# Two fp32 load pairs split into partition halves over two DMA queues, and four more output stores cut in two, in a fused channel-attention and MLP kernel

## The chip, the cores and the metric

The kernel runs on one core of a Trainium2 chip. The metric is device time in microseconds (us) of that core, as the median of several executions. The kernel before takes 713.97 us (three executions, 713.9 to 714.35); the profiled execution has a span of 712.6 us.

## What is computed

Channel attention (XCiT style) over four batches of 6080 tokens and 256 channels, and then a two-layer MLP with a squared-ReLU activation over all 24,320 tokens.

```python
qn = q / (norm(q, axis=1) + 1e-6);  kn = k / (norm(k, axis=1) + 1e-6)   # norms over the 6080 tokens
s  = kn.T @ qn / tau                       # 256 x 256 for each batch
a  = softmax-like exp(s - max) / sum       # per row
x  = v @ a                                 # (24320, 256)
h  = x @ w_in                              # 256 -> 2048
out = (s * relu(h)**2 + b) @ w_out         # 2048 -> 256, fp32
```

Inputs and outputs are fp32. The products on the chip are done in fp16 with fp32 accumulation.

## The kernel before, in words

**Two phases.** The attention matrix of a batch is folded into the first MLP weight (`wa = a @ w_in`, one 256 x 2048 matrix for each batch), so that the tokens pass through two matrix products only. A batch's matrix needs all its tokens of q and k. For batch 0 nothing can hide that: q and k are loaded, their Gram matrix and norms are summed, the softmax and the fold are done, and only then does the token loop start. I call this stretch the head. The token loop goes over `NG` = 48 groups of 512 tokens (the last has 256); the Gram matrices of batches 1 to 3 are computed inside it.

**The head.** Batch 0 is cut into 13 chunks: eleven of 128 partitions x 4 rows, one of 128 x 2 and one of 96 x 2. A chunk has a k and a q part, each 512 KB of fp32 in memory for a full chunk. `Gram.load` (L119) issues them. For the first `NDIRECT` = 2 chunks the parts go uncast into the fp32 tile `raw32` (L131): k on SyncE's queue, q on ScalarE's queue. `Gram.cast` (L136) then converts them to fp16 into the chunk's `qk` tile: k on VectorE (L139), q on ScalarE (L140). All other chunks are issued on GpSimd's queue (L133), where the transfer itself casts to fp16. `qk_pool` has eight buffers. Behind the loads of batch 0 GpSimd's queue has the first group of v (L453), the pieces of w_in (L512), and then w_out and more of v.

For each chunk TensorE does eight matmuls into `s_ps` (L149), which need both parts of the chunk. Squares of k and q are taken on ScalarE (L180) and VectorE (L177), folded on VectorE (L194) and summed into one row block (L208). The last three chunks (`NLATE` = 3) are handled apart: k's squares first, then the norms by ones-matmuls (L247, L251), the inverse norms on ScalarE (L272), the scaling of `s_ps` (L297), the exponentials (L303), the fold of the first weight columns (L347, L324, L326). The first matmul of the token loop is `h_ps` (L751). `keep_busy` (L544) adds a few idle matmuls late in the head.

**The token loop.** A group has 16 steps. Each step does two matmuls of the first product (L751); its result is taken out by ScalarE as ReLU (L761) and squared on VectorE or ScalarE (L774, L772). The second product of a group runs one group later: seven products of half size in place of eight (`seven_items`, L922), with sums of blocks on VectorE (L849 to L855). VectorE scales and adds the result into `o_sb` (L779), and `store` (L786) sends it to memory on SyncE's queue. v is loaded by GpSimd (L453) and transposed by DMA on SyncE's queue (L475), some 26 steps before its use.

**Order.** Every compute instruction and most transfers are kept in program order on their engine. The two direct loads (L131) are not, but nothing waits ahead of them: each stands at the start of its queue. A `store` waits on SyncE's queue until VectorE has written its part of `o_sb`, and the transposes of a later group of v stand behind it.

**Stores.** In `p3` and `p4` of `seven_items`, a group in `HALVES` (L838) is stored in two parts: columns of rows 0 and 1 of each partition after the sixth product, rows 2 and 3 after the seventh. Any other group is stored in one transfer after the seventh. Both kinds cover all 128 partitions.

Of the kernel before, what the change touches and what calls it, by code (L numbers as in the profile page):

```python
# [17 lines left out]
def kernel(  # L18
# [12 lines left out]
    nc = tc.nc  # L31
    P = 128
# [16 lines left out]
    NG = (NT + TG - 1) // TG  # L49
# [6 lines left out]
    def po(ins):  # L56

        tc.keep_in_program_order(ins)
        return ins
# [52 lines left out]
    class Gram:  # L112
# [7 lines left out]
        def load(self, c, parts=(0, 1)):  # L120

            at, np_, jc = self.chunks[c]
            if 0 in parts:
                self.raw[c] = qk_pool.tile([P, 2, JC, C], FP16, tag="qk", name="qk")
            t = self.raw[c]
            direct = self.b == 0 and c < NDIRECT
            for i in parts:
                src = (k, q)[i]
                rows = src[self.b, at : at + np_ * jc, :].rearrange("(p j) c -> p j c", j=jc)
                if direct:  # L130
                    (nc.sync, nc.scalar)[i].dma_start(out=raw32[:, c, i], in_=rows)  # L131
                else:
                    po(nc.gpsimd.dma_start(out=t[:np_, i, :jc, :], in_=rows))  # L133
            self.tiles[c] = t[:, 1], t[:, 0]
# [356 lines left out]
    raw32 = gpool.tile([P, NDIRECT, 2, JC, C], FP32, tag="g16", name="raw32")  # L491
# [166 lines left out]
    for i, f in enumerate(folds):  # L658
        early.setdefault(FOLDS[i], []).append(f)
    at_step(14, lambda: po(nc.vector.tensor_scalar_mul(  # L660
        out=s_out, in0=s_bc, scalar1=1.0 / (LAM * LAM))))
# [114 lines left out]
    def evacuate(dst, src, add, n):  # L776
        if n == 1:
            add = add[:, None, :].broadcast_to((P, 2, add.shape[-1]))
        po(nc.vector.scalar_tensor_tensor(out=dst, in0=src, scalar=s_out, op0=ALU.mult,  # L779
                                          in1=add, op1=ALU.add))  # L780

    def store(g, j0=0, j1=None, cols=slice(0, C), queue=nc.sync):
        t0, nj = group(g)
        o_sb = o_sbs.pop(g) if j1 is None else o_sbs[g]
        j1 = nj if j1 is None else j1
        po(queue.dma_start(  # L786
            out=out[t0 : t0 + nj * P, :].rearrange("(p j) d -> p j d", j=nj)[:, j0:j1, cols],
            in_=o_sb[:, j0:j1, cols]))
# [46 lines left out]
                    store(g)  # L835


    HALVES = (1, 2, 3, NG - 2)  # L838
    S = {}

    def sums_of(g, n, i0=0, i1=NP):
# [15 lines left out]
    def seven_items(g):  # L857
# [6 lines left out]
        def out_sb(t, half):  # L864
            if g not in o_sbs:
                o_sbs[g] = opool.tile([P, TG // P, C], FP32, tag="o_sb", name="o_sb")
            return o_sbs[g][:, ts(t, 2), half]
# [19 lines left out]
        def p3():  # L887
            evacuate(out_sb(0, hi), st["Z"], st["u2"], 2)
            if g in HALVES:
                store(g, 0, 2)  # L890

        def p4():
            evacuate(out_sb(1, lo), st["X"], rowconst[:, lo], 1)
            store(g, 2 if g in HALVES else 0)

# [123 lines left out]
```

## Time and profile before

| | value |
|---|---|
| time, median of 3 | 713.97 us |
| span of the profiled execution | 712.6 us |
| busy TensorE, VectorE, ScalarE, GpSimd | 97%, 89%, 77%, 16% |
| first matmul of the head | 7.56 us |
| first matmul of the token loop | 37.59 us |
| DMA busy share, 0 to 60 us | 0.9 or more from 2 us on |
| moved by DMA in the whole span | 83.81 MB |
| store, 512 KB, SyncE's queue: issue to landing | 3.0 us (43 of them) |
| store, 256 KB, SyncE's queue: issue to landing | 5.9 us (8 of them) |

The busy shares are means over the whole span. The head and the token loop have different limits, so the views are read for each of them apart. In the view of the chain that ended last, each line is a start, a duration and what filled it; in the view of waits, each line is who waited, for whom, the sum in us, the number of waits and the longest.

### The profile page before, as it was taken

The numbers are of one execution on the slowest core, as the hardware profiler recorded it, in microseconds if no ns is written. First come the engines' busy times: TensorE is split into PE (matmuls) and PEld (weight loads), VectorE is DVE, ScalarE is ACT, GpSimd is POOL, SyncE is SP. The second block draws the span as 40 slices with busy tenths as digits, with TensorE's granted clock in tenths as the row PEclk, the third lists the DMA queues.
The fourth block names the chain that finished last, engine by engine and source line by source line (L and its number), as shares of the span: only waits on it lengthen the run. The fifth ranks groups of instructions, "written<-read, shape, count | busy, mean of one in ns | idle before, by whom it ended". The sixth has DMA issues, their size and how long they took to land.

```text
span 712.6 us, 17529 instructions
## 1 busy us (share of the span) xinstructions
PE 693.7 (97%) x7422; PEld 502.7 (71%) x7422; DVE 635.1 (89%) x905; ACT 548.8 (77%) x599; POOL 113.7 (16%) x192
## 2 busy tenths in 40 slices
PE   3799999999999999999999999999999999999998
PEld 2556777776777777777677777777768777777777
DVE  4889999999988989998999899998998888888886
ACT  5789877787777777778877777777876777777875
POOL 4533042202101222111010222111000000000000
PEclk9899999999999999999999999999999999999999
DMA  9999998557655977465761889737323333321202
GB/s 234 207 258 174 166 176 140 111 105 122 128 113 105 138 139 147 106 96 101 153 130 50 149 136 148 128 76 99 99 64 75 95 71 75 97 61 46 83 31 75
DMA packets 87838, 83.81 MB, mean 118 GB/s; under 512 B 56352, under 2 KB 62768, under 8 KB 87760
## 3 DMA queue, kind: packets, MB, share of 16 engines
q0 software_dynamic: 26992, 43.74, 38.2%
q1 hardware_dynamic: 60192, 37.71, 22.1%
q8 instruction: 58, 0.95, 0.5%
q10 hardware_dynamic: 576, 1.25, 0.5%
q14 instruction: 20, 0.16, 0.1%
HBM read 78.91 MB, written 24.90 MB: 146 GB/s over the span
## 4 chain that ended last, share of the span: by engine, by line
PE 95%; DMA 3%; ACT 1%; DVE 1%; issue 0%; DVEq 0%; ACTq 0%
PE h_ps L751 46%; PE o_ps L922 40%; PE s_ps L149 4%; DMA qk<-in_k_dram 1%; PE wa_ps L389 1%; DMA raw<-in_q_dram 1%; PE o_ps L826 1%; ACT sq L180 1%; PE o_ps L798 0%; PE wa_ps L331 0%; DVE f L194 0%; ACT r L272 0%; PE n_ps L247 0%; ACT qk L140 0%; DVE f L208 0%
## 5 line engine op out<-in xcount | busy, mean ns | idle before, releaser
L761 ACT ACTIVATE r<-h_ps 128x1024 f16<-128x1024 f32 (+1 forms) x384 | 388.8, 1014 | 143.8 <-PE h_ps L751 140.3
L751 PE MATMUL h_ps<-vT,wa 128*128 128x512 f16 (+7 forms) x1632 | 452.0, 364 | 0.5 <-ACT wa L324 0.5
L922 PEld LDWEIGHTS <-S 128*128 128x128 f16 x2944 | 198.1, 98 | 84.3
L922 PEld LDWEIGHTS <-g 128*128 128x128 f16 x2208 | 155.0, 98 | 74.0
L774 DVE TENSOR_TENSOR g<-r 128x2048 f16<-128x2048 f16 (+2 forms) x150 | 174.4, 1163 | 10.2 <-ACT r L761 9.7
L922 PE MATMUL o_ps<-T,S 128*128 128x128 f16 x2208 | 183.1, 219 | 0.0
L751 PEld LDWEIGHTS <-wa 128*128 128x128 f16 x1632 | 136.6, 98 | 19.0 <-ACT wa L324 1.0
L922 PE MATMUL o_ps<-w_out,g 128*128 128x128 f16 x1472 | 134.2, 219 | 0.0
L772 ACT ACTIVATE g<-r 128x1024 f16<-128x1024 f16 (+1 forms) x97 | 100.3, 1034 | 0.2
L779 DVE SCALAR_TENSOR_TENSOR o_sb<-o_ps,s_out,u 128x256 f32<-128x256 f32 x138 | 66.2, 480 | 36.1 <-PE o_ps L922 34.3
L149 PE MATMUL s_ps<-qk 128*128 128x256 f16 (+1 forms) x384 | 71.8, 289 | 13.9 <-ACT qk L140 9.4
L453 POOL DMA_DIRECT2D v<-in_v_dram x48 | 31.4, 663 | 238.7 <-DMA vT<-v 173.8
L210 POOL DMA_DIRECT2D f<-f x33 | 28.9, 875 | 248.4 <-DVE f L194 201.5
L779 DVE SCALAR_TENSOR_TENSOR u<-o_ps,s_out,rowconst 128x256 f32<-128x256 f32 x138 | 65.7, 476 | 0.0
L922 PE MATMUL o_ps<-w_out,S 128*128 128x128 f16 x736 | 63.5, 219 | 0.0
L922 PE MATMUL o_ps<-N,g 128*128 128x128 f16 x736 | 63.4, 219 | 0.0
L180 ACT ACTIVATE sq<-qk 128x1024 f16<-128x1024 f16 (+2 forms) x53 | 54.5, 1041 | 3.9 <-DMA qk<-in_k_dram 2.4
L851 DVE TENSOR_TENSOR S<-S,g 128x2048 f16<-128x2048 f16 (+1 forms) x47 | 56.4, 1200 | 1.2
L849 DVE TENSOR_TENSOR S<-g 128x2048 f16<-128x2048 f16 (+1 forms) x47 | 56.0, 1192 | 0.0
L855 DVE TENSOR_TENSOR S<-g,S 128x2048 f16<-128x2048 f16 x46 | 55.9, 1214 | 0.0
L853 DVE TENSOR_TENSOR S<-g 128x2048 f16<-128x2048 f16 x46 | 55.8, 1214 | 0.0
L149 PEld LDWEIGHTS <-qk 128*128 128x128 f16 (+1 forms) x384 | 32.9, 103 | 20.4 <-ACT qk L140 9.9
(103 smaller groups left out, 335.1 us busy)
## 6 DMA issues: line engine op xcount, KB each, us to landing
out_dram<-o_sb SPq DMA_DIRECT2D x43, 512.0 KB, 3.0
v<-in_v_dram POOLq DMA_DIRECT2D x47, 256.0 KB, 4.6
qk<-in_k_dram POOLq DMA_DIRECT2D x42, 256.0 KB, 6.4
qk<-in_q_dram POOLq DMA_DIRECT2D x42, 256.0 KB, 7.1
f<-f POOLq DMA_DIRECT2D x30, 128.0 KB, 3.0
vT<-v SPq DMA_TRANSPOSE x182, 3.1
w<-in_moe_w_out_dram POOLq DMA_DIRECT2D x4, 512.0 KB, 9.8
out_dram<-o_sb SPq DMA_DIRECT2D x8, 256.0 KB, 5.9
```

Source lines behind the costliest of these rows:

```text
L149: po(nc.tensor.matmul(self.s_ps[:, ch, :], qc[:np_, j, ts(ch, P)], kc[:np_, j, :], start=(c == 0 and j == 0 and ch == 0), stop=(c == len(s ...
L180: po(nc.scalar.activation(out=st["sq"][:np_, a, js, :], in_=(qc, kc)[a][:np_, js, :], func=AF.Square))
L751: po(nc.tensor.matmul(dst, wa[:, ci, ts(m, P)], src, start=(ci == 0), stop=(ci == CH - 1), skip_group_check=True))
L761: po(nc.scalar.activation(out=r16[:, :, i % 2, :n], in_=h_tiles.pop((g, i))[:, :, :n], func=AF.Relu))
L772: po(nc.scalar.activation(out=dst, in_=src, func=AF.Square))
L774: po(nc.vector.tensor_mul(dst, src, src))
L779: po(nc.vector.scalar_tensor_tensor(out=dst, in0=src, scalar=s_out, op0=ALU.mult, in1=add, op1=ALU.add))
L849: po(nc.vector.tensor_add(T[1], A21, A22))
L851: po(nc.vector.tensor_sub(T[2], T[1], A11))
L853: po(nc.vector.tensor_sub(T[3], A11, A21))
L855: po(nc.vector.tensor_sub(T[4], A12, T[2]))
L922: po(nc.tensor.matmul(st[name][:, j, :], a()[:, i, ts(j, P)], w[:, i, :], start=first, stop=last, skip_group_check=True))
```

## The change

```diff
                 if direct:
-                    (nc.sync, nc.scalar)[i].dma_start(out=raw32[:, c, i], in_=rows)
+                    for h, queue in enumerate((nc.sync, nc.scalar)):
+                        ps = ts(h, P // 2)
+                        queue.dma_start(out=raw32[ps, c, i], in_=rows[ps])
                 else:
                     po(nc.gpsimd.dma_start(out=t[:np_, i, :jc, :], in_=rows))
...
-    HALVES = (1, 2, 3, NG - 2)
+    HALVES = (*range(1, 8), NG - 2)
```

The first edit touches the four direct loads (k and q of chunks 0 and 1). Each 128-partition transfer of 512 KB becomes two of 64 partitions and 256 KB: partitions 0 to 63 on SyncE's queue, 64 to 127 on ScalarE's. A queue that carried k of chunk 0 and k of chunk 1 now carries halves of k0, q0, k1, q1 in this order. Its aim is that both queues work on the part that is needed first. The casts now each wait for two transfers.

The second edit puts groups 4 to 7 among the groups whose store goes out in two transfers of 256 KB. Its aim is that the first half leaves earlier, and that the store is shorter for the transposes behind it on the queue.

Instructions of TensorE, VectorE and GpSimd are the same in number and order. ScalarE's and SyncE's queues have the added transfers.

## Prediction

> **What bounds the kernel now.** I looked first at TensorE's waits over the whole span (who waits, for whom: us in total, times, longest).
>
> ```profile
> PE s_ps L149 <- ACT qk L140: 9.4, 2, 7.6
> PE s_ps L149 <- DMA qk<-in_q_dram: 4.5, 6, 1.5
> PE n_ps L247 <- DVE half L224: 1.3, 1, 1.3
> PE h_ps L751 <- ACT wa L324: 0.5, 1, 0.5
> PE r_ps L342 <- ACT eT L303: 0.3, 1, 0.3
> ```
>
> All of them lie in the head, before the first `h_ps` matmul at 37.59 us; asked for the span from 38 us on, the same view names no wait of TensorE. Ends of matmuls are modelled, so I looked at starts in the timeline:
>
> ```profile
> 100.21 0.59 PE L751 MATMUL h_ps<-vT,wa 128*128 128x512 f16 x2
> 100.64 0.55 PE L922 MATMUL o_ps<-T,S 128*128 128x128 f16 x7
> 101.03 0.59 PE L751 MATMUL h_ps<-vT,wa 128*128 128x512 f16 x2
> ```
>
> Two matmuls of 512 columns take 0.43 us from start to start (215 ns each), seven of 128 take 0.39 us (56 ns each). Over all matmul starts of the trace after 60 us these spacings hold from the 1st to the 99th percentile (215 to 216 ns, 55 to 56 ns), and after 38 us only two spacings are over 80 ns too long, 0.2 us together. So from 37.6 us to the end TensorE runs its stream without a hole: about 675 us that depend on neither loads nor stores. Only the head can be shortened, and it can be lengthened.
>
> The chain that ended last, in the head (start, us, what):
>
> ```profile
> 1.19 9.00 DMA raw<-in_q_dram
> 10.21 1.05 ACT qk L140
> ...
> 20.75 9.46 DMA qk<-in_k_dram
> ...
> 37.59 0.61 PE h_ps L751 x2
> ```
>
> It goes through the second chunk's q, ScalarE's cast and squares, and a late k load. Whether the loads are late because they are issued late or because the DMA engines are full is told by busy time in stretches of 2 us (last columns: TensorE's clock, DMA share, GB/s):
>
> ```profile
> 4.00:6.00 2.00, 0.00 (x0) 0.00 (x0) 0.00 (x0) 0.00 (x0) 1.81 (x4) 1.00 1.02 409
> 8.00:10.00 2.00, 1.45 (x7) 0.73 (x5) 0.14 (x1) 0.00 (x0) 0.00 (x0) 1.00 1.12 271
> 12.00:14.00 2.00, 2.00 (x11) 1.45 (x10) 1.11 (x2) 2.00 (x3) 0.76 (x2) 1.00 1.12 210
> 30.00:32.00 2.00, 0.74 (x5) 0.39 (x4) 1.80 (x5) 1.64 (x3) 1.51 (x3) 1.00 1.18 208
> ```
>
> All 16 engines are busy from 2.5 us on. The uncast raw loads move 409 GB/s. The casting loads write 208 GB/s and read twice that, 416 GB/s of fp32. q and k of batch 0 are 12.45 MB; at 0.413 MB/us from 2.5 us on they are in at 32.6 us, and the last q parts are in fact waited for at 32.6 to 33.8 us. The head is bound by DMA throughput, and the order in which its loads are served does not move its end: a later GpSimd load lands 9.5 us after its issue because some eight are queued ahead of it.
>
> [...] The packet records of this trace agree: from 6 to 8 us SyncE's, ScalarE's and GpSimd's queues advance about one to one to one. [...] The trace before has no 64-partition transfer[...].
>
> **The change part by part.**
>
> *Stores of groups 4 to 7.* Four more issues of about 0.34 us (L786 in the timeline) on SyncE's queue, which spends 370 us waiting for VectorE at that line. The first half waits for the sixth product, the second for the seventh, where the whole store waited before: nothing behind it is held longer. Transposes land some 3.1 us after issue and are used about 26 steps later. TensorE waits for none of this. I cost it at 0.0, and hide it behind the TensorE stream.
>
> *The direct loads, if the engines keep their rate.* Four issues of about 0.4 us per queue in place of two; they are over by 2.5 us, before the first chunk lands. 64 added completion packets of 9 to 22 ns over 16 engines: under 0.1 us. k0 and k1 land sooner, by my estimate at 5.1 and 8.1 us against 6.28 and 9.86. But matmuls need q as well, and q0 and q1 come when both queues have moved 1 MB and 2 MB together, as now: 6.4 and 10.2 us. ScalarE's cast of q1 keeps its place ahead of its squares. So nothing on the path moves: 0.0, hidden behind the same bytes.
>
> [...] The raw packets are 4096 bytes in 159 ns (packet records), 25.8 GB/s for an engine. [...] Each engine has 32 such packets (2.1 MB / 4096 / 16). [...] I take +3.0 us[...]. As the head is throughput-bound and later GpSimd loads queue on the same engines, this delay passes to its end in full; the free capacity to catch up isn't there (share 1.1 to 1.2 throughout).
>
> Sum: 0.0 + 0.0 + 3.0, so 714.0 + 3.0 = 717.0 us.
>
> **Rivals.**
>
> *No change, 714.0 us.* For it: bytes and packet sizes are equal; both halves are in flight together[...]. Against: ScalarE's first packets start 0.5 us after SyncE's (2.29 against 1.79 us), so at first all engines work on the same half[...]. Small shifts of up to 0.5 us either way belong here: the first, cold packets take 350 to 1460 ns and could come out differently.
>
> *Faster, 712.3 us.* The chain read literally: the head's second chunk sets the pace, and if its k part, 1.7 us earlier, freed VectorE and then everything behind it, the whole 1.7 us would come. Against: the chain starts at q1, not k1; and issue doesn't limit the loads, throughput does.
>
> *Slower for another reason, 716 us.* TensorE's granted clock is 0.5 from 20.9 to 27.8 us, where it costs little as chunks come only every 2.5 us. If other gaps move that stretch by 6.8 us onto the exit of the head, some 1.8 us of TensorE work on the chain there (norm sums, 0.95 us, and as much of q's sums and last Gram matmuls) runs at half speed: +1.8.
>
> **How the numbers follow.** [...]0.57 (717.0[...]), no change 0.33 (713.5 to 714.6), clock shift 0.05 (716), faster 0.05 (712.3). Slower by over 0.2% (715.4) is the first and the third, 0.62; same 0.33; faster 0.05. [...]713.6 to 718.8 leaves out the fast rival and the ends of the others, under 2 in 10.
>
> **What would show it.** [...]the stretch from 4 to 6 us falls from 409 towards 210 to 300 GB/s, raw packets take over 200 ns, ScalarE's cast of q1 starts at 12 us or later in place of 10.21, the first `h_ps` matmul at about 40.6 us in place of 37.59, and the 675 us after it are unchanged. No change: k's casts come 1 to 1.7 us earlier, q's do not move, first `h_ps` at 37.3 to 37.9 us. I'd be wrong in the steps if TensorE showed a wait after 38 us (stores matter), or if the first `h_ps` came over 1 us earlier (the head isn't bound by throughput).

## The result, and the profile after

The changed kernel takes 718.06 us (six executions, 717.26 to 718.76) where the kernel before takes 714.02 us beside it (713.88 to 714.96). The ratio is 1.0055, with a 95% interval of 1.0042 to 1.0068: 4.0 us slower. The profiled execution has a span of 715.9 us, 3.3 us over the 712.6 of before. It is one of the two with a mean granted TensorE clock of 1.00, and these took 717.26 and 717.74 us; the three at 0.995 took 717.95 to 718.76. So what follows explains 3.3 us; the rest is taken up under the clock rival.

TensorE's waits over the whole span, in the kernel after (who, for whom: us in total, times, longest):

```profile
PE s_ps L151 <- ACT qk L142: 13.5, 2, 10.6
PE s_ps L151 <- DMA qk<-in_q_dram: 4.6, 4, 1.2
PE n_ps L249 <- DVE half L226: 2.1, 1, 2.1
PE r_ps L344 <- ACT eT L305: 0.6, 1, 0.6
PE h_ps L753 <- ACT wa L326: 0.5, 1, 0.5
```

The wait for the two casts of q has grown from 9.4 to 13.5 us. All five waits still lie in the head: asked from 41 us on, the view has only the last of them, which ends at 40.87 us. The first `h_ps` matmul starts at 40.87 us in place of 37.59, and from there to the end it is 675.0 us in both profiles. So the whole difference lies in the head. The casts of chunks 0 and 1 in the timeline after:

```profile
5.58 0.75 DVE L141 CAST qk<-raw 128x1024 f16<-128x1024 f32 x1 [3.87 <-DMA raw<-in_k_dram]
9.47 1.04 ACT L142 CAST qk<-raw 128x1024 f16<-128x1024 f32 x1 [7.45 <-DMA raw<-in_q_dram]
11.96 0.69 DVE L141 CAST qk<-raw 128x1024 f16<-128x1024 f32 x1 [5.64 <-DMA raw<-in_k_dram]
14.29 1.04 ACT L142 CAST qk<-raw 128x1024 f16<-128x1024 f32 x1 [3.78 <-DMA raw<-in_q_dram]
```

Before, they started at 6.28, 6.46, 9.86 and 10.21 us. k of chunk 0 comes 0.7 us earlier, as the change meant. All else is later: q0 by 3.0, k1 by 2.1, q1 by 4.1 us. One stretch of 2 us gives a first hint (last columns: TensorE's clock, DMA share, GB/s):

```profile
4.00:6.00 2.00, 0.00 (x0) 0.00 (x0) 0.42 (x1) 0.00 (x0) 1.81 (x4) 1.00 0.95 203
```

From 4 to 6 us the engines are nearly as busy as before (0.95 against 1.02), but write 203 GB/s in place of 409. This mixes two things, and the records of single DMA packets tell them apart:

- The raw packets (the uncast loads' 512 packets of 4096 bytes) take longer. Those that start from 2.9 us on, so that the slow first ones don't count, have a mean of 237 ns in place of 165. Over all 512, an engine spends 7.71 us on its raw packets in place of 6.05.
- GpSimd's casting loads come in earlier, from 4.1 us on in place of 5.5. Their packets write half of what they read; 70 of them start between 4 and 6 us, where before it was 7. By the end of the last raw packet 337 of them have been served in place of 184, which is 3.71 us of an engine's time in place of 1.98.

The last raw packet ends at 13.2 us in place of 9.7. Of these 3.5 us, longer packets make 1.7 and GpSimd's packets that went ahead another 1.7. The cast of q1 then starts 1.1 us after the last raw packet, where before it was 0.5.

The chain that ended last has changed its kind, too (start, us, what):

```profile
2.91 11.30 DMA raw<-in_q_dram
14.29 1.04 ACT qk L142
...
16.20 0.87 ACT sq L182
17.15 1.05 ACT sq L182
18.22 0.70 DVE f L196
18.95 0.44 DVE f L196
19.41 0.43 DVE f L210
19.84 0.61 DVE sq L179
...
34.73 0.35 DVE half L226
35.12 0.95 PE n_ps L249 x7
```

The late k load that stood in the chain of before, at 20.75 us, is gone. From 18.2 to 35.1 us the chain is VectorE's squares and folds, one after the other. VectorE's waits from 18 to 38.5 us agree:

```profile
DVE sm_t L299 <- PE s_ps L151: 1.4, 1, 1.4
DVE f L196 <- ACT sq L182: 0.7, 1, 0.7
```

The 0.7 us lie at 18.2 us and the 1.4 us at 38.35, after the norms. Between them VectorE never waits: it has become the limit of the head.

### The profile page after: what moved, and what is told of

Read it like the earlier page. It is cut to its first block, busy times and chain, and to the rows that moved or that the text cites. A ratio compares the mean times of both kernels' runs of the same rounds, so it can differ in the third digit from the quotient of the medians.

```text
span 715.9 us, 17552 instructions
## 1 busy us (share of the span) xinstructions
PE 691.8 (97%) x7422; PEld 502.4 (70%) x7422; DVE 635.0 (89%) x905; ACT 548.7 (77%) x599; POOL 113.7 (16%) x192
## 3 DMA queue, kind: packets, MB, share of 16 engines
q10 hardware_dynamic: 608, 1.25, 0.7%
## 4 chain that ended last, share of the span: by engine, by line
PE 94%; DVE 2%; DMA 2%; ACT 1%; issue 0%; ACTq 0%; DVEq 0%
PE h_ps L753 46%; PE o_ps L924 40%; PE s_ps L151 4%; DMA raw<-in_q_dram 2%; DVE f L196 1%; PE wa_ps L391 1%; PE o_ps L828 1%; PE o_ps L800 0%; DVE f L210 0%; PE wa_ps L333 0%; ACT r L274 0%; DVE sq L179 0%; ACT sq L182 0%; ACTq L133 0%; PE n_ps L249 0%
## 5 line engine op out<-in xcount | busy, mean ns | idle before, releaser
L151 PE MATMUL s_ps<-qk 128*128 128x256 f16 (+1 forms) x384 | 70.5, 285 | 18.1 <-ACT qk L142 13.5
```

The costliest lines, as they stand in the source:

```text
L151: po(nc.tensor.matmul(self.s_ps[:, ch, :], qc[:np_, j, ts(ch, P)], kc[:np_, j, :], start=(c == 0 and j == 0 and ch == 0), stop=(c == len(s ...
```

## The experiments

Each experiment ran beside the kernel before; "before" in a ratio is the kernel before on the same chip. To compare heads I read three instants from each timeline: the start of ScalarE's cast of q1, the start of the first w_in load on GpSimd's queue (it stands behind a wait for one of the late q parts, so it tells when these land), and the first `h_ps` matmul.

```
kernel                     us     cast q1  w_in issue  first h_ps   h_ps-cast  h_ps-w_in
before                   714.0     10.21     29.26       37.59        27.38      8.33
stores only              714.2      9.73     28.79       37.11        27.38      8.32
before, less VectorE     714.0      9.87     28.93       37.26        27.39      8.33
before, 512 KB more      715.3      9.75     30.03       38.37        28.62      8.34
split by rows            715.2     11.46     29.22       38.02        26.56      8.80
chunk 0 split            716.4     12.31     29.80       38.89        26.58      9.09
loads only               717.4     13.65     30.83       40.22        26.57      9.39
after                    718.1     14.29     31.78       40.87        26.58      9.09
both queues one half     718.9     14.32     31.33       40.90        26.58      9.57
loads only, less VectorE 716.0     13.49     30.63       38.90        25.41      8.27
chunks 2, 3 in halves    715.8     10.47     29.43       38.99        28.52      9.56
chunks 2, 3 by rows      714.3      9.49     29.34       37.67        28.18      8.33
```

Starts shift by up to 0.5 us between profiles of unchanged raw loads, which is why differences of instants are used. The two kernels with chunks 2 and 3 cut come last in this section.

In the expectations, theory A is the main case of the prediction: the raw packets of a transfer of one partition half are longer, and this costs the time. It was my estimate; no trace of before has such a transfer.

**Which edit costs the time.** Loads alone:

```diff
-    HALVES = (*range(1, 8), NG - 2)
+    HALVES = (1, 2, 3, NG - 2)
```

> Only the loads of chunks 0 and 1 are split into partition halves; the stores are as before. Theory A[...]: about 718 us, as with both edits, raw packets of some 240 ns on the mean in place of 165. Rival S (the stores cost the time): 714 us.

717.4 us, ratio 1.0053 [1.0040, 1.0065]; raw packets 234 ns on the mean from 2.9 us on. Stores alone:

```diff
-    HALVES = (1, 2, 3, NG - 2)
+    HALVES = (*range(1, 8), NG - 2)
```

> Only groups 4 to 7 are stored in halves; the loads are as before. Theory A: 714.0 us, no wait of TensorE after 38 us. Rival S: about 718 us.

714.19 us, ratio 1.0003 [0.9994, 1.0011], and no wait of TensorE after 38 us. The stores cost and bring nothing that these runs resolve; the interval of the loads alone overlaps that of the whole change.

**The partition halves, or more transfers in another order.** The same number of transfers, on the same queues in the same order, but cut along the rows of each partition:

```diff
-                        ps = ts(h, P // 2)
-                        queue.dma_start(out=raw32[ps, c, i], in_=rows[ps])
+                        js = ts(h, JC // 2)
+                        queue.dma_start(out=raw32[:, c, i, js], in_=rows[:, js])
```

> As many transfers as in the change, of the same bytes, on the same queues and in the same order (k0, q0, k1, q1, one part on each queue), but each part has all 128 partitions and two of the four rows of a partition, so packets are 2048 bytes. Stores as before. Theory A: [...]two packets of 2048 bytes together take hardly more than one of 4096 took (159 ns), cast of q1 on ScalarE at about 10.2 us, total 714.0 to 714.6 us. Rival N (more transfers, their order, or two queues for one part cost the time): 717 us or more.

715.17 us, ratio 1.0017 [1.0011, 1.0024]. The median packet of 2048 bytes took 84 ns, so two of them take 168 ns for what one did in 159: no stretching. But it isn't free, as theory A had expected, nor does it cost the 717 us of rival N. In its timeline the second of these lines is q1's cast:

```profile
6.25 1.04 ACT L142 CAST qk<-raw 128x1024 f16<-128x1024 f32 x1 [4.23 <-DMA raw<-in_q_dram]
11.46 1.04 ACT L142 CAST qk<-raw 128x1024 f16<-128x1024 f32 x1 [4.16 <-DMA raw<-in_q_dram]
29.22 0.74 POOL L514 DMA_DIRECT2D w_in<-in_moe_w_in_dram  x1 [0.78 <-DMA qk<-in_q_dram]
```

q1 is 1.25 us later than before though the late loads land at the same time (29.22 against 29.26). An engine's time on raw packets is unchanged (6.07 us against 6.05), but 287 of GpSimd's packets were served before the last raw one, where before it was 184: 1.1 us of an engine's time, nearly all of the 1.2 us by which the last raw packet is later. In the two half microseconds from 7 to 8 us the queues of SyncE, ScalarE and GpSimd got 24, 26, 23 and 24, 23, 26 packets, where before they got 16, 16, 16 and 17, 16, 17. So the queues take turns by packet here, whatever its size, and the raw queues lose bytes when their packets are small.

Both halves of k on SyncE's queue and both of q on ScalarE's, so that both queues work on the same half:

```diff
-                    (nc.sync, nc.scalar)[i].dma_start(out=raw32[:, c, i], in_=rows)
+                    for h in range(2):
+                        ps = ts(h, P // 2)
+                        (nc.sync, nc.scalar)[i].dma_start(out=raw32[ps, c, i], in_=rows[ps])
```

> Loads split into partition halves, but both halves of k stay on SyncE's queue and both halves of q on ScalarE's, in the order low half, high half. Stores as before. Now both queues work on the same half at the same time. Theory A: [...]mean of 280 to 300 ns, cast of q1 at 14 to 15 us, total 718.5 to 720 us, at or above the change. Rival N (order or two queues for one part): k and q are on their own queues again, so 714 to 715 us.

718.92 us, ratio 1.0070 [1.0056, 1.0084]. The cast of q1 at 14.32 us is as theory A has it; packets are slower than in the change, 254 ns, but not 280 to 300. k and q are on their own queues again, and yet it is no faster than the change. So it is the halves that stretch the packets, and not the sharing of a part by two queues; more transfers of smaller packets, as the cut by rows has them, cost 1.2 us in another way. In the stretch from 4 to 6 us it reads

```profile
4.00:6.00 2.00, 0.00 (x0) 0.00 (x0) 0.00 (x0) 0.00 (x0) 1.81 (x4) 1.00 1.02 213
```

**A smaller dose.** Chunk 0 alone is split, chunk 1 is loaded whole:

```diff
                     for h, queue in enumerate((nc.sync, nc.scalar)):
+                        if c > 0:
+                            if h == i:
+                                queue.dma_start(out=raw32[:, c, i], in_=rows)
+                            continue
                         ps = ts(h, P // 2)
```

> Only chunk 0 is split into partition halves; chunk 1 is loaded whole, k on SyncE's and q on ScalarE's queue. Stores as before. Theory A: [...]q1 later by half of the 3.4 to 4.1 us, cast at about 12.0 us, first h_ps at 12.0 + 26.57 = 38.6 us, total 715.0 us. Rival N (a fixed cost of any split): 717 us or more, or 714.

716.36 us, ratio 1.0033 [1.0020, 1.0045]. The cast of q1 at 12.31 us and the first `h_ps` at 38.89 us are near the 12.0 and 38.6 expected; the time is 1.4 us over the 715.0 expected, and only part of that is in the head. q1 is late by 2.1 us, about half of the 4.1 of the change, so its delay follows the number of halved transfers. In the packet records the whole transfers of chunk 1 go at means of 159 and 172 ns on the two queues again from 9 to 10.5 us.

**What carries the delay to the end of the head.** The last two columns of the table hold two constants. In the first four kernels, whose raw loads are untouched, the first `h_ps` comes 8.32 to 8.34 us after the w_in issue. In the next five, where q1 is late, it comes 26.56 to 26.58 us after q1's cast, though the distance from the w_in issue goes from 8.80 to 9.57. So the head seems to end with the later of two chains: the last q parts from memory, and VectorE's work behind the cast of q1. Three runs test this. First, VectorE's folds of chunks 1 and 3 left out:

```diff
+            if self.b == 0 and c in (1, 3):
+                return ops
             ops += [fold(2, slice(0, 2), False), fold(1, slice(0, 2), True)]
```

with the split loads:

> The split loads alone, and VectorE's three folds of chunk 1 and of chunk 3 left out (3.06 us of VectorE; the norms lack these two chunks, so the output is not the reference's). The profiles so far fit: first h_ps = the later of (start of the cast of q1 + 26.57 us, VectorE without a gap) and (GpSimd's wait for the late q loads to land + 8.33 us). Theory V (with q1 late, VectorE's chain sets the end of the head): VectorE's term falls by 3 us, the loads' term is then the later one, 1.0 us under e1: 716.4 us. Rival T (the lateness of the loads alone sets it, as predicted): unchanged, 717.4 us.

and in the kernel before:

> The kernel before with the same folds of chunks 1 and 3 left out (output not the reference's). If the head of the kernel before is bound by its loads: unchanged, 714.0 us. If VectorE's chain bounds it there too: up to 3 us less, 711 us.

With the split loads: 715.99 us, ratio 1.0027 [1.0016, 1.0038], against 1.0053 [1.0040, 1.0065] with the folds. 1.4 us came back (1.3 in the first `h_ps`, 1.0 expected), though the loads are hardly faster. At a mean granted clock of 0.998 or more the loads alone took 716.95 to 717.40 us and this kernel 715.62 to 716.66, so it isn't the clock. Its chain has the late k load again, and not VectorE:

```profile
22.10 9.46 DMA qk<-in_k_dram
31.56 0.02 issue
31.59 1.06 ACT sq L182
```

In the kernel before, the same 3.06 us of VectorE taken away give nothing: 714.01 us, ratio 1.0000 [0.9992, 1.0008]. Then, 512 KB more on GpSimd's queue of the kernel before:

```diff
+    extra = late_pool.tile([P, JC, C], FP16, tag="extra", name="extra")
     for c in range(NDIRECT, len(g0.chunks) - NLATE):
         g0.load(c)
+        if c == 3:
+            po(nc.gpsimd.dma_start(
+                out=extra, in_=v[3, :P * JC, :].rearrange("(p j) c -> p j c", j=JC)))
```

> The kernel before with one more casting load of 512 KB (v, into a tile that nobody reads) on GpSimd's queue behind chunk 3. It stands behind the raw loads, so the cast of q1 stays at 10.2 us. If throughput bounds the head before: eight more packets of 173 ns on each engine, +1.4 us, 715.4 us. If the chain from q1 bounds it: 714.0 to 714.4 us.

715.34 us, ratio 1.0017 [1.0010, 1.0024]: +1.3 us, where 1.4 was expected from throughput, with the cast of q1 no later than before.

```profile
9.75 1.05 ACT L140 CAST qk<-raw 128x1024 f16<-128x1024 f32 x1 [2.75 <-DMA raw<-in_q_dram]
30.03 0.74 POOL L516 DMA_DIRECT2D w_in<-in_moe_w_in_dram  x1 [0.70 <-DMA qk<-in_q_dram]
38.37 0.60 PE L755 MATMUL h_ps<-vT,wa 128*128 128x512 f16 x2 [0.48 <-ACT wa L324]
```

So the head of the kernel before is bound by DMA throughput, and that of the kernel after by VectorE behind q1.

**Halves with half the writing rate.** A raw packet writes 25.8 GB/s (4096 bytes in 159 ns), a casting packet 11.9 (2048 bytes in 172 ns). Theory A is here, again as my estimate, that halves get longer packets at the raw rate only. Chunks 2 and 3, which cast, split on GpSimd's queue:

```diff
-                    po(nc.gpsimd.dma_start(out=t[:np_, i, :jc, :], in_=rows))
+                    halves = 2 if self.b == 0 and c in (2, 3) else 1
+                    for h in range(halves):
+                        ps = ts(h, np_ // halves)
+                        po(nc.gpsimd.dma_start(out=t[ps, i, :jc, :], in_=rows[ps]))
```

> The raw loads are as before; the four casting loads of chunks 2 and 3 on GpSimd's queue are split into partition halves (0 to 63, then 64 to 127). Such packets write only 2048 bytes in 172 ns, 11.9 GB/s[...]. Theory A[...]: packets stay at 172 to 180 ns, total 714.0 to 714.5 us. Rival N (a transfer of 64 partitions is slow in itself): packets of 230 ns or more and 715.5 us or more.

Their packets stay at 172 to 173 ns, as theory A has it; but the time is 715.80 us, ratio 1.0022 [1.0013, 1.0032], as the rival had it. The last q part is late, which the chain shows:

```profile
25.65 9.23 DMA qk<-in_q_dram
34.88 0.02 issue
34.90 0.77 DVE sq L180 x2
```

In the waits of these last microseconds VectorE's squares wait up to 1.4 us for it, where before the longest was 0.2. In these traces a load's landing shows as 16 steps of a semaphore. For this load, 15 come by 33.39 us, and the last at 34.88; before, all 16 were there by 33.30. Up to then the last two steps of every load lie at most 0.2 us apart, those of the halved loads too. The DMA view from 32.5 to 34.5 us shows what came between:

```profile
q8 instruction: 1, 0.02, 3.0%
```

It is one packet of 16,384 bytes on the queue that the profile calls "instruction", from 32.86 us on for 0.98 us. In the eleven other profiles it starts between 35.16 and 38.88 us, when the last q parts are in. So the 1.8 us of this run don't show a cost of the halves: the late sixteenth step goes with that packet, but whether the packet held it up, and why it came earlier here, is not on record.

Two things the run does show. The halved casting packets read 4096 bytes in 172 ns, where a raw packet took 159, and write half; they don't stretch, so a limit on the reading side is unlikely (argued from this run, on another queue). And the raw packets beside them do stretch, though they belong to whole transfers: the 41 from 8 us on have a mean of 222 ns, where before it is 168 (61 packets). The same number of added transfers, cut along the rows instead:

```diff
-                        ps = ts(h, np_ // halves)
-                        po(nc.gpsimd.dma_start(out=t[ps, i, :jc, :], in_=rows[ps]))
+                        js = ts(h, jc // halves)
+                        po(nc.gpsimd.dma_start(out=t[:np_, i, js, :], in_=rows[:, js]))
```

> As many added transfers on GpSimd's queue for chunks 2 and 3 as with partition halves there, but each part has all 128 partitions and two of the four rows (1024 bytes written a packet, about 98 ns by the late chunks' packets, so 2 x 98 in place of 173 ns: 16 x 2 x 23 ns = 0.7 us more engine time at most). If the added transfers themselves made the last q part late in the run with partition halves: 715.8 us or more again. If the partition halves did it[...]: the packets' own 0.3 to 0.7 us only, 714.3 to 714.8 us, and no straggling engine.

714.30 us, ratio 1.0002 [0.9994, 1.0010], with the end of the head 8.33 us after the w_in issue. So the added transfers alone cost nothing that this run resolves. But its instruction packet starts at 35.65 us, behind the last q part, so the two runs differ in more than the cut, and they don't single out the halves.

## Why the prediction was right, and where it was not

**Where the time would change: right.** TensorE has no wait in its stream, which takes 675.0 us from the first `h_ps` in both profiles, and the stores cost 0.0 (ratio 1.0003).

**Longer raw packets: right in kind.** Raw packets took over 200 ns, 203 GB/s were written from 4 to 6 us, q1's cast started beyond 12 us, and the first `h_ps` came at 40.87 us where 40.6 was named. Two queues did not make up for the halves: the mean raw packet grew from 165 to 237 ns. That is a factor of 1.4, where the prediction's 210 to 300 GB/s in place of 409 are factors of 1.9 to 1.4; the 203 GB/s are no test of it, since GpSimd's packets are in them. What the runs show is that halved raw loads have longer packets, and that halved loads with half the writing rate don't (172 to 173 ns). Why the raw ones get longer was not shown.

**One premise of the rival of no change was half wrong.** It argued that both halves are in flight together. Up to 6 us they mostly took turns: from 2.5 to 3 us all 34 raw packets are SyncE's, from 3.5 to 4 us all 32 ScalarE's, and from 4.5 to 6 us 47 are SyncE's and 4 ScalarE's. But from 6.5 to 12 us both deliver side by side (130 and 151 packets), and these packets still take 236 ns on the mean, where before they took 166. So it isn't the turns alone that cost. Nor is one half at a time always slow: the 48 packets that SyncE's queue started from 2.5 to 3.5 us took 176 ns, and why these were spared is open. With both queues on the same half, the time was 0.9 us above that of the change, with intervals that overlap.

**The size came out near, in part by luck.** The prediction's +3.0 us stands against +3.3 in the profiles and +4.0 between the medians. It was my estimate of the stretching, and no trace had shown any. In the profile the stretching is 1.7 us of an engine's time on the mean. GpSimd's packets add as much: 153 more of them went ahead of the last raw packet, another 1.7 us. Then 0.8 us were hidden at the end of the head. The errors nearly cancel.

**The step that failed** is how the delay reaches the end of the head: "As the head is throughput-bound and later GpSimd loads queue on the same engines, this delay passes to its end in full". The late loads were 2.5 us later (w_in issue at 31.78 in place of 29.26; 1.6 us in the profile of the loads alone), while q1 was 4.1 us later, since GpSimd's packets had gone ahead of it. If the late loads set the end, it would have come 8.33 us after the w_in issue, at 40.11 us. It ended at 40.87, by VectorE's chain, 26.58 us after q1's cast. The kernel before had 0.8 us of room there: 10.21 + 26.57 = 36.78 against the measured 37.59. A q1 that is 4.1 us late costs 4.1 - 0.8 = 3.3 us, which is what the profiles show. The sentence that the order of the loads "does not move its end" fails with it: the cut by rows left an engine's raw time as it was, changed who was served first, and cost 1.2 us. The rival "chain read literally" had the right chain for a late q1, and the wrong sign: an earlier k1 could bring nothing, since before it is the loads that end last, as 714.01 us with less VectorE work shows.

**The clock rival** did not act in the profiled execution: its granted clock is 1.00 in every stretch of the head. But it may act in the others. The three kernels with all four raw loads halved took 717.26 and 717.74 (the change), 716.95 and 717.12 (loads only), 718.10 and 718.49 us (both queues one half) at a mean clock of 1.00, and 717.95 to 718.76, 718.54 and 718.80, and 718.92 to 719.40 us at 0.995: medians 0.9 to 1.6 us higher. In the kernel before, 0.995 and 1.00 differ by 0.2 us. The prediction had named 1.8 us for a lowered clock at the exit of the head. No slower-clock execution of the change has a trace, so where it loses the time is not shown.

No version here beats the kernel before.

## What to carry to other kernels

Cutting uncast loads like these into partition halves for two queues brought the first part 0.7 us sooner and all others 2 to 4 us later. The cut into halves cost 3.4 us here (717.4 in place of 714.0), a cut of the same loads along the free dimension 1.2 (715.2). So keep all 128 partitions in each piece of loads like these; if a piece must be smaller, cut along the free dimension, and count what smaller packets lose against other queues. Where a stretch has two chains that end nearly together, take the room of each (here 0.8 us) from instants in several runs before saying that a delay passes in full or is hidden; a single chain of waits shows only the later one. And before a cost is put down to an edit, look in the packet records for what else moved: here one instruction packet.

## What the runs showed of the hardware that was not expected

- Half of q1's delay was not slower packets. Of the 3.5 us by which the last raw packet was later, 1.7 came from GpSimd's packets that were served ahead of it.
- Halving the packets of the raw loads to 2048 bytes made q1 1.25 us later beside GpSimd's packets, at nearly the same time per byte (84 ns against 159 for 4096).
- Halved casting loads left their own packets at 172 to 173 ns, while raw packets of whole transfers beside them went from 168 to 222 ns.
- An instruction packet of 16,384 bytes took 0.98 us. Where it ran ahead of the last q part's landing, the last of that load's 16 semaphore steps came 1.5 us after the fifteenth.
- Issuing a 64-partition transfer took 0.57 to 0.86 us on ScalarE's and SyncE's queues. Two whole ones took 0.87 us together in the kernel before, and one of all 128 partitions with half the rows 0.39 to 0.46. But the whole ones of chunk 1, behind the halves of chunk 0, took 0.58 and 0.60.
- The kernel after varies more: 717.26 to 718.76 us, with 713.88 to 714.96 before. Its four slower executions, 717.95 us and up, are those with a mean clock of 0.995 to 0.998, and the two at 1.00 took 717.26 and 717.74.
